# A third buffer for the conversion of a float64 weight, and a later place for the routing's constants

## The chip, the cores and the metric

The kernel runs on one core of a Trainium2 chip. The metric is the device time of one execution in microseconds; of several executions the median counts. The core has TensorE (matmuls into PSUM), VectorE, ScalarE and GpSimd for the work beside them, and SyncE, whose queue issues nearly all transfers of this kernel. Each engine takes its instructions in the order in which the program holds them.

## What is computed

Three blocks follow each other: an attention with a threshold, a dense two-layer block, and a routed block with 8 experts of which each token takes one.

```python
# attention: 4 x 8 heads, 576 positions, 64 wide; then x is [2304, 512]
scores = np.where(scores >= max(scores) - tau, scores, -1e9)
x = softmax(scores) @ v
# dense block, w_in [512, 2048], w_out [2048, 512], both float64 in memory
h = x @ w_in
g = np.where(h > 0, h, np.exp(np.minimum(h, 0)) - 1)
x = g @ w_out
# routed block, 8 experts, 512 -> 1024 -> 512
logits = x @ w_gate + modality_bias[modality_id]
e = argmax(logits); out = softmax(logits)[e] * (relu(x @ w1[e]) @ w2[e])
```

## The kernel before

The work is cut into three programs that follow each other: attention with the first dense layer (`Phase1`), the second dense layer with the routing (`Phase2`), and the experts (`Experts`). In the first two an order is worked out before the kernel is built: each step goes into a `Plan` with an engine, a cost, a due time, the steps it needs and the buffers it uses, and `Plan.order` lets a clock run over them. The step whose due time is earliest and whose buffer is free comes next on its engine. A ring (`pl.ring(tag, n)`) says how many buffers of a kind there are. The planner's times are only there to find an order; on the chip the engines take that order and wait for each other by semaphores.

High precision comes from splitting: a float32 operand becomes a high part and the remainder, and three matmuls stand for one product.

The change is in `Phase2`, in the stretch between the attention and the token stage. Four things run there side by side.

- **Units.** The first dense layer of the last batch: 32 units (two halves for each of 16 chunks of 128 hidden features), which I number 96 to 127 as the whole kernel counts them. A unit is 12 matmuls into one of six PSUM banks `u` (line 715), two ScalarE steps (`eh`: 727 and 731), one VectorE step (`g`: 734), which frees the bank, and a store of `g` to memory `gD` (738, 144 KB).
- **Conversion of w_out** (`convert`, chunk c = 0 to 15). w_out lies in memory as float64; a chunk is 128 rows, 512 KB. SyncE loads it (1152) into a buffer `gr`, of which there are two. VectorE makes a float32 pattern from the two halves of the bits (1162 and 1163, the bit steps), ScalarE the sign (1169) and the absolute value (1171), VectorE the product (1172), ScalarE the high part in `WB` (1174), VectorE the remainder (1175). The buffer is free again when 1163 and 1169 have read it.
- **Constants** (`constants`). Two groups share one buffer `stg`: the modality bias (two small loads at 1121 and 1122, VectorE 1128 to 1133), and the matrices for counting tokens (GpSimd iotas at 1096 to 1099, VectorE 1103 to 1108, then stores at 1112 to 1116: 128 KB to a table, one row, and three stores of 256.5 KB of zeros).
- **First pieces of g for the tokens** (`tokens`). There are 18 tiles of 128 tokens. Each takes its g in two halves of 8 feature chunks: a load of 512 KB into a buffer `gr` (1201), ScalarE's high part (1206), GpSimd's remainder (1210), then 24 matmuls (1227) of the 48 of a tile. Loads of g and chunks of w_out share the ring `gr`.

After the 18 tiles come the leading expert, whose rows are gathered into `XG0`, a tile of 128 x 2 x 513 floats that nothing uses before, and the other experts.

Of the kernel before, what the change touches and what calls it, by code (L numbers as in the profile page):

```python
# [11 lines left out]
I32 = mybir.dt.int32  # L12
# [195 lines left out]
class Phase1:  # L208
# [15 lines left out]
    def pools(self, ctx, xa, xb, tp):  # L224
        nc, tc, pl, o = self.nc, self.tc, self.pl, self.opt
        self.xa, self.xb, self.tp = xa, xb, tp
        pool = lambda name, bufs, **k: ctx.enter_context(tc.tile_pool(name=name, bufs=bufs, **k))
        one, self.wk, self.sm = pool("a1", 1), pool("awk", 1), pool("asm", 4)
        self.ps_s, self.ps_h = pool("ps_s", 2, space=PSUM), pool("ps_h", 4, space=PSUM)
        self.bufs = dict(s=2, h=4, e=2, p=o["p"], tf=2, th=2, tl=2, pvl=1, xo=o["xo"], R=1, qr=1, kr=1, ql=1,  # L230
                         vr=2, vs=2, kh=2, kl=2, q0=2, q1=2, eh=2, g=4, r=1, xha=1, xhb=1, w=1, wf=1, sums=4)
        for tag, n in self.bufs.items():
            pl.ring(tag, n, tag in ("vr", "vs", "q0", "q1"))
        self.ntau = one.tile([128, 1], F32, name="ntau")
        self.QS = [one.tile([128, 1280], F32R, name=f"QS{i}") for i in range(2)]

        self.VR = [one.tile([128, 5, 128], F32, name=f"VR{i}") for i in range(2)]
        self.VS = [one.tile([128, 5, 2, 64], F32R, name=f"VS{i}") for i in range(2)]
        for t in self.QS:
            nc.vector.memset(t[:, 576:640].bitcast(F32), 0.0)  # L240
# [815 lines left out]
class Phase2:  # L1056
# [14 lines left out]
    def pools(self, ctx, keep, xa, xb, tp):  # L1071
        tc, pl = self.tc, self.pl
        self.xa, self.xb, self.tp = xa, xb, tp
        one = self.one = keep.enter_context(tc.tile_pool(name="k1", bufs=1))
        pool = lambda name, bufs, **k: ctx.enter_context(tc.tile_pool(name=name, bufs=bufs, reuse_waits="tile", **k))
        self.sm, self.wk = pool("msm", 3), pool("gwk", 2)
        self.pu, self.pc = pool("ps_u", 6, space=PSUM), pool("ps_c", 1, space=PSUM)
        for tag, n in dict(u=6, xt=1, pr=1, xw=2, eh=2, g=4, gr=2, gs=2, stg=1, xrow=3, ht=1).items():
            pl.ring(tag, n, tag in ("gs", "ht", "xw"))
        self.XT0 = one.tile([128, 2, KT, 256], F32R, name="xt0")  # L1080
        self.XG0 = one.tile([128, 2, XW], F32, name="xg0")
        self.IDX = [one.tile([128, 24], I32, name=f"idx{i}") for i in range(2)]
        self.GT = [one.tile([128, 2], F32, name=f"gt{i}") for i in range(2)]
# [58 lines left out]
    def convert(self, c, t0, free):  # L1142

        nc, pl, T = self.nc, self.pl, self.T
        d = t0 + c * self.opt["wstep"]
        br = pl.new("gr")

        sl = c % 4 if c < 12 else 2 + c % 2

        def load():  # L1150
            T["w64", c] = self.wk.tile([128, 512, 2], I32, name="gr", tag="gr")
            nc.sync.dma_start(T["w64", c].rearrange("p a t -> p (a t)"), self.wsrc[:, c, :])

        raw = lambda w: T["w64", c][:, :, w]
        wf = lambda s: T["w64f"][sl // 2][:, sl % 2, s]
        dst = [self.WO[:, s, c, :] for s in range(2)]

        def bits():
            if c == 0:
                T["w64f"] = [self.xa.tile([128, 2, 2, 512], F32, name="w64f", tag=x, bufs=1) for x in ("xh", "xl")]  # L1160
            A = wf(0).bitcast(I32)
            nc.vector.tensor_scalar(A, raw(1), 0x08000000, 3, op0=ALU.bitwise_xor, op1=ALU.logical_shift_left)
            nc.vector.scalar_tensor_tensor(A, raw(0), 29, A, op0=ALU.logical_shift_right, op1=ALU.bitwise_or)

        ml = self.opt["wmul"](c)
        k0 = pl.dma(1456, 1, d - 4000, load, [], [br])
        before = self.slot.get(sl, [])
        k1 = pl.op("D", 1140, d, bits, [k0] + self.k_conv + before, [br], after=free, port=True)
        k2 = pl.op("A", 520, d, lambda: nc.scalar.activation(wf(1), raw(1).bitcast(F32), AF.Sign), [k0, *([k1] if c == 0 else []), *self.k_conv, *before], [br], after=free)
        self.k_conv = self.k_conv or [k1]  # L1170
        k3 = pl.op("A", 520, d + 1000, lambda: nc.scalar.activation(wf(0), wf(0), AF.Abs), [k1])
        k4 = pl.op(ml, 600 if ml == "D" else 1230, d + 1500, lambda: (nc.vector if ml == "D" else nc.gpsimd).tensor_tensor(
            wf(0), wf(0), wf(1), op=ALU.mult), [k2, k3], port=True)
        k5 = pl.op("A", 520, d + 2800, lambda: nc.scalar.copy(dst[0], wf(0)), [k4])
        k6 = pl.op("D", 600, d + 3300, lambda: nc.vector.tensor_tensor(dst[1], wf(0), dst[0].bitcast(F32), op=ALU.subtract),
                   [k5], port=True)
        self.slot[sl] = [k5, k6]
        self.wdone[c] = [k5, k6]
# [370 lines left out]
    def run(self):  # L1549
        o, pl, ph = self.opt, self.pl, self.ph  # L1550
        p1 = ph.pl
        t0 = max(p1.free["PE"], 0)
        self.wdone, self.l1mm, self.put3, self.k_w0, self.k_table, self.k_x = {}, [], [], [], [], []
        self.k_place = None
        self.k_conv = []
        self.slot = {}
        kneed = [max(p1.done(x) for x in y) for y in ph.xdone[B - 1]]
        tL = t0 + o["l1gap"]
        for u in range(2 * FC):
            self.l1mm.append(ph.unit(pl, B - 1, u, tL + 1464 * u, "u", self.pu, self.tp, [], kneed, []))  # L1560
            self.put3.append(len(pl.ops) - 1)
        self.constants(t0 + 10000)
        free = max(p1.done(k) for k in ph.last_mm)
        for c in range(FC):
            self.convert(c, t0 + o["w0"], free)
        t2 = tL + 1464 * 2 * FC
        self.gate_weights(t2)
        for i in range(TT):
            self.tokens(i, t2 + STEP * i)
            if i == PREDICT:  # L1570
                k = self.k_e0 = self.first(t2 + STEP * i + 18500)
                for c in range(8):
                    self.weights(c, k, t2 + STEP * i + 22000 + o["ew"] * c)
            if i == SNAP:
                self.begun(t2 + STEP * i + 18500)
        self.lead(t2 + STEP * TT)
        with self.tc.manual_schedule():
            pl.emit()
# [67 lines left out]
```

## Time and profile before

| | us |
|---|---|
| median of 3 runs | 1043.26 (1043.04 to 1044.56) |
| the profiled execution, its own time | 1040.67 |
| its span in the profile | 1038.7 |
| TensorE busy | 987.1 (95%) |
| VectorE busy | 633.5 (61%) |
| ScalarE busy | 566.5 (55%) |
| GpSimd busy | 472.2 (45%) |

The page gives shares over the whole span; a change in one stretch is read from that stretch. The units of the last batch run from 467 to 532 us of the span, the conversion of w_out from 471 to 536, the tokens from 533 to about 780, the experts from there to the end. In a timeline row the first number is the start, the second the duration of the group; in square brackets stands the idle time of the engine before it and what ended that. Consecutive instructions of one engine overlap a little at their ends, so their cost to the engine is the distance from one start to the next.

### The profile page before, as it was taken

The numbers are of one execution on the slowest core, as the hardware profiler recorded it, in microseconds if no ns is written. First come the engines' busy times: TensorE is split into PE (matmuls) and PEld (weight loads), VectorE is DVE, ScalarE is ACT, GpSimd is POOL, SyncE is SP. The second block draws the span as 40 slices with busy tenths as digits, with TensorE's granted clock in tenths as the row PEclk, the third lists the DMA queues.
The fourth block names the chain that finished last, engine by engine and source line by source line (L and its number), as shares of the span: only waits on it lengthen the run. The fifth ranks groups of instructions, "written<-read, shape, count | busy, mean of one in ns | idle before, by whom it ended". The sixth has DMA issues, their size and how long they took to land. (4 is left out here: it accounts for less than half of the span.)

```text
span 1038.7 us, 17784 instructions
## 1 busy us (share of the span) xinstructions
PE 987.1 (95%) x6241; PEld 864.3 (83%) x6241; DVE 633.5 (61%) x1574; ACT 566.5 (55%) x1183; POOL 472.2 (45%) x346
## 2 busy tenths in 40 slices
PE   8999899899999999998889999999999998999993
PEld 7666698899999999998778888877888897888982
DVE  6878899998989897856851222243444653464431
ACT  5777899899999999976762222333221211121000
POOL 3444787787667667541024444477523210211110
PEclk9999999999999999999999999999999999999997
DMA  5544454434424332116863333355312520441111
GB/s 174 152 121 128 118 152 132 123 117 118 131 88 123 99 111 70 59 64 199 227 211 113 105 104 103 114 153 172 112 41 83 200 65 24 141 122 53 41 44 25
DMA packets 107538, 117.75 MB, mean 113 GB/s; under 512 B 11920, under 2 KB 83872, under 8 KB 107426
## 3 DMA queue, kind: packets, MB, share of 16 engines
q1 hardware_dynamic: 102930, 104.00, 33.8%
q0 software_dynamic: 4496, 12.35, 3.9%
q8 instruction: 59, 0.97, 0.4%
q14 instruction: 53, 0.43, 0.1%
HBM read 80.36 MB, written 29.85 MB: 106 GB/s over the span
## 5 line engine op out<-in xcount | busy, mean ns | idle before, releaser
L1227 PE MATMUL u<-WB,gs 128*128 128x512 f32 x864 | 216.1, 402 | 3.7 <-POOL gs L1210 2.6
L1227 PEld LDWEIGHTS u<-WB,gs 128*128 128x128 f32 x864 | 158.4, 189 | 39.5 <-POOL gs L1210 3.7
L480 POOL TENSOR_TENSOR tl<-tf,th 128x512 fp32r<-128x512 f32 (+1 forms) x120 | 145.3, 1215 | 80.8 <-ACT tf L477 80.3
L715 PE MATMUL h<-xh,WA 128*128 128x288 f32 x768 | 172.4, 300 | 0.9 <-DVE g L734 0.5
L715 PEld LDWEIGHTS h<-xh,WA 128*128 128x128 f32 x768 | 128.8, 189 | 3.6 <-DVE g L734 1.9
L1210 POOL TENSOR_TENSOR gs<-gr,gs 128x1024 fp32r<-128x1024 f32 x36 | 87.1, 2420 | 95.2 <-ACT gs L1206 95.1
L419 DVE SCALAR_TENSOR_TENSOR p<-s,a,e 128x576 f32<-128x576 f32 x144 | 116.5, 813 | 19.5 <-ACT e L409 12.8
L397 DVE TENSOR_REDUCE a<-s 128x1 f32<-128x576 f32 x144 | 107.4, 753 | 16.4 <-PE s L386 14.1
L715 PE MATMUL h<-xl,WA 128*128 128x288 f32 x384 | 113.2, 295 | 0.0
L409 ACT ACTIVATE e<-s,a 128x576 f32<-128x576 f32 x144 | 106.8, 745 | 8.3 <-DVE a L397 6.4
L430 PE MATMUL h<-ident,p 128*128 128x128 f32 x576 | 87.8, 276 | 6.3 <-DVE p L419 4.9
L877 ACT CAST xtr<-px 128x512 fp32r<-128x512 f32 x16 | 9.4, 588 | 150.3 <-issue 85.2
L1258 DVE TENSOR_TENSOR lg<-xt,bt 128x8 f32<-128x8 f32 x18 | 3.0, 166 | 135.3 <-PE xt L1254 135.3
L820 POOL DMA_INDIRECT out<-o,idx x16 | 17.7, 1104 | 144.6 <-DVE o L932 101.3
L386 PE MATMUL s<-kh,QS 128*128 128x288 f32 x320 | 79.8, 331 | 1.4 <-DVE p L419 0.8
L430 PEld LDWEIGHTS h<-ident,p 128*128 128x128 f32 x576 | 68.8, 141 | 11.5 <-DVE p L419 4.7
L715 PEld LDWEIGHTS h<-xl,WA 128*128 128x128 f32 x384 | 72.6, 189 | 0.0
L386 PE MATMUL s<-kl,QS 128*128 128x288 f32 x320 | 69.1, 298 | 0.6 <-POOL kl L300 0.6
L1206 ACT CAST gs<-gr 128x1024 fp32r<-128x1024 f32 x36 | 37.8, 1049 | 56.5 <-issue 35.3
L471 ACT CAST th<-h 128x512 fp32r<-128x512 f32 (+1 forms) x120 | 64.0, 542 | 4.5 <-PE h L430 3.5
L477 ACT COPY tf<-h 128x512 f32<-128x512 f32 (+1 forms) x120 | 64.6, 546 | 1.4
L715 PE MATMUL u<-xh,WA 128*128 128x288 f32 x256 | 55.6, 306 | 8.6 <-DVE g L734 8.3
(207 smaller groups left out, 2083.7 us busy)
## 6 DMA issues: line engine op xcount, KB each, us to landing
gD<-g SPq DMA_DIRECT2D x128, 144.0 KB
gr<-gD SPq DMA_DIRECT2D x36, 512.0 KB
stg<-w SPq DMA_DIRECT2D x24, 512.0 KB
kr<-kP SPq DMA_DIRECT2D x30, 288.0 KB
w<-w_in SPq DMA_DIRECT2D x16, 512.0 KB
gr<-w_out SPq DMA_DIRECT2D x16, 512.0 KB
VR<-v SPq DMA_DIRECT2D x16, 320.0 KB
x2D<-xrow SPq DMA_DIRECT2D x18, 256.5 KB
```

What stands on the lines that cost most here:

```text
L386: nc.tensor.matmul(s[:, hf, 0:288], q, k[:, 288 * hf:288 * hf + 288], start=(m == 0), stop=(m == len(mm) - 1))
L397: nc.vector.tensor_reduce(T["a", i][:, 0:1], T["s", i][:, :, 0:288], axis=AX.XY, op=ALU.max, negate=True)
L409: nc.scalar.activation(e, T["s", i][:, :, 0:288], AF.Exp, bias=T["a", i][:, 0:1])
L419: nc.vector.scalar_tensor_tensor(p, T["s", i][:, :, 0:288], T["a", i][:, 1:2], T["e", i], op0=ALU.is_ge, op1=ALU.mult, accum_out=T["sums", ...
L430: nc.tensor.transpose(tp[:, 128 * c:128 * c + 128], pf[:, 128 * c:128 * c + 128], self.ident)
L471: a1 = op("A", ta(4), de, lambda src=src, dst=dst: nc.scalar.copy(dst("th"), src()), [k5], [bT])
L477: nc.scalar.copy(f[:, :, 0:w], src())
L480: nc.gpsimd.tensor_tensor(dst("tl"), T["tf", i, g][:, :, 0:w], dst("th").bitcast(F32), op=ALU.subtract)
L715: nc.tensor.matmul(T["h", key], self.WIN[:, s, kt, fc * 128:fc * 128 + 128], x[:, kt, q], start=(kt == 0 and j == 0), stop=(kt == KT - 1 a ...
L1206: nc.scalar.copy(T["gs", n % 2][:, 0], T["gr", n])
L1210: nc.gpsimd.tensor_tensor(g[:, 1], T["gr", n], g[:, 0].bitcast(F32), op=ALU.subtract)
L1227: nc.tensor.matmul(T["x2", i], T["gs", n][:, a, f % 8, :], self.WO[:, b, f, :], start=(f == 0 and j == 0), stop=(f == FC - 1 and j == 2))
```

## The change

The ring of buffers for chunks of w_out gets a third member for every third chunk (c = 2, 5, 8, 11, 14): the tile `XG0`, which later takes the leading expert's rows, is viewed as 1024 integers for each partition. In the plan the loads of chunks are due 4 us earlier and are counted as 1.5 us longer. The constants' due time moves from 10 to 46 us after the start of the stretch.

```diff
-        for tag, n in dict(u=6, xt=1, pr=1, xw=2, eh=2, g=4, gr=2, gs=2, stg=1, xrow=3, ht=1).items():
+        for tag, n in dict(u=6, xt=1, pr=1, xw=2, eh=2, g=4, gr=2, gs=2, stg=1, xrow=3, ht=1, xg=1).items():
...
-        br = pl.new("gr")
+
+        third = c % 3 == 2
+        br = pl.new("xg" if third else "gr")
...
         def load():
-            T["w64", c] = self.wk.tile([128, 512, 2], I32, name="gr", tag="gr")
+            if third:
+                T["w64", c] = self.XG0.rearrange("p a b -> p (a b)")[:, 0:1024].bitcast(I32).rearrange("p (a t) -> p a t", t=2)
+            else:
+                T["w64", c] = self.wk.tile([128, 512, 2], I32, name="gr", tag="gr")
             nc.sync.dma_start(T["w64", c].rearrange("p a t -> p (a t)"), self.wsrc[:, c, :])
...
-        k0 = pl.dma(1456, 1, d - 4000, load, [], [br])
+        k0 = pl.dma(1456, 1, d - 8000, load, [], [br], extra=1500)
...
-        self.constants(t0 + 10000)
+        self.constants(t0 + 46000)
```

The planner's order on TensorE stays as it was. On the others it changes within this stretch. In the kernel after the change the lines from 1152 on are numbered 5 higher (a load of a chunk is 1157, of g 1206).

SyncE's queue at the start of the conversion, before (`gr<-w_out` is the load of a chunk, `gD<-g` the store of a unit, `tabD` and the stores that follow it the constants):

```order
L1152 DMA gr<-w_out 128x1024 x2
L1121 DMA stg<-mod 128x18x2
L1122 DMA stg<-bias 128x16
L1184 DMA wg<-w_gate 128x4x8
L738 DMA gD<-g 128x288
L1152 DMA gr<-w_out 128x1024
L738 DMA gD<-g 128x288
L1152 DMA gr<-w_out 128x1024
L738 DMA gD<-g 128x288 x2
L1152 DMA gr<-w_out 128x1024
L738 DMA gD<-g 128x288 x2
L1152 DMA gr<-w_out 128x1024
```

and now (`xg` is the third buffer):

```order
L1157 DMA gr<-w_out 128x1024 x2
L1157 DMA xg_6987<-w_out 128x1024
L1121 DMA stg<-mod 128x18x2
L1122 DMA stg<-bias 128x16
L1189 DMA wg<-w_gate 128x4x8
L738 DMA gD<-g 128x288 x3
L1157 DMA gr<-w_out 128x1024 x2
L738 DMA gD<-g 128x288
L1157 DMA xg_6987<-w_out 128x1024
```

Chunk 2 is loaded right behind chunks 0 and 1, ahead of the small loads; chunk 3 stands behind three stores where chunk 2 stood behind one. Before, the constants' stores came right behind the last row shown, ahead of chunk 6.

The same queue at the end of the conversion, now, from the load of chunk 15 on:

```order
L1157 DMA gr<-w_out 128x1024
L738 DMA gD<-g 128x288
L1206 DMA gr<-gD 128x8x128
L738 DMA gD<-g 128x288 x4
L1206 DMA gr<-gD 128x8x128
L738 DMA gD<-g 128x288 x2
L1206 DMA gr<-gD 128x8x128
L738 DMA gD<-g 128x288 x2
L1112 DMA tabD<-stg 128x256
L1113 DMA x2D<-stg 1x513
L1116 DMA x2D<-stg 128x513 x3
L738 DMA gD<-g 128x288 x3
```

The constants' stores now stand behind the first three loads of g. The first load of g takes the buffer of chunk 13 (before: chunk 14's), the second the same buffer again once GpSimd has read it (before: chunk 15's), the third that of chunk 15.

VectorE behind the bit steps of chunk 15 (1167 and 1168), now:

```order
L1167 TENSOR_SCALAR w64f<-gr 128x512
L1168 SCALAR_TENSOR_TENSOR w64f<-gr,w64f 128x512
L1128 CAST stg<-stg 128x18
L1130 TENSOR_SCALAR stg<-stg 128x18
L1131 TENSOR_TENSOR bt<-stg 128x144
L1130 TENSOR_SCALAR stg<-stg 128x18
L1131 TENSOR_TENSOR stg<-stg 128x144
L1133 TENSOR_TENSOR bt<-bt,stg 128x144
L734 SCALAR_TENSOR_TENSOR g<-eh,u 128x288 x2
L1180 TENSOR_TENSOR WB<-w64f,WB 128x512
L1177 TENSOR_TENSOR w64f<-w64f 128x512
```

Before, the six rows of the bias stood behind the product of chunk 0, and the second group (1103 to 1108) behind the bit steps of chunk 3; that group now stands behind the remainder of chunk 15. The first of the two unit steps shown (734) is unit 121's, which frees the bank for unit 127, the last.

ScalarE at the same place, now:

```order
L727 ACTIVATE eh<-u 128x288
L1211 CAST gs<-gr 128x1024
L1174 ACTIVATE w64f<-gr 128x512
L1179 CAST WB<-w64f 128x512
L731 ACTIVATE eh<-eh 128x288
L1176 ACTIVATE w64f<-w64f 128x512
```

The cast of the first half of g (1211) now stands ahead of the sign of chunk 15 and of unit 121's exponential (731). Before, it stood behind the absolute value of chunk 15, one unit later.

## Rows read from the trace of the kernel before

**Rows 1.** Stretches: us, busy of PE, PEld, DVE, ACT, POOL, PEclk, DMA share, GB/s.

```profile
490.00:500.00 10.00, 7.19 (x48) 6.49 (x48) 6.34 (x13) 6.04 (x13) 0.00 (x0) 1.00 1.06 236
500.00:510.00 10.00, 8.33 (x51) 8.33 (x52) 9.50 (x19) 9.50 (x21) 0.00 (x0) 0.83 0.85 260
510.00:520.00 10.00, 9.22 (x65) 8.52 (x64) 9.01 (x18) 8.62 (x19) 0.00 (x0) 1.00 0.75 232
...
580.00:780.00 200.00, 197.15 (x998) 160.22 (x999) 65.64 (x308) 60.29 (x104) 102.74 (x54) 1.00 0.37 114
```

**Rows 2.** Waits from 466 to 540 us: us in total, times, longest.

```profile
ACT w64f L1169 <- DMA gr<-w_out: 8.9, 7, 3.4
PE u L715 <- DVE g L734: 8.3, 9, 3.9
```

**Rows 3.** Timeline of SyncE's queue: zeros, chunks 6 and 8, first and third g.

```profile
489.50 1.36 SPq L1116 DMA_DIRECT2D x2D<-stg  x3
...
491.82 0.63 SPq L1152 DMA_DIRECT2D gr<-w_out  x1
...
501.33 0.33 SPq L1152 DMA_DIRECT2D gr<-w_out  x1
...
525.88 0.37 SPq L1201 DMA_DIRECT2D gr<-gD  x1
...
535.19 0.37 SPq L1201 DMA_DIRECT2D gr<-gD  x1
```

**Rows 4.** Timeline of VectorE: chunk 0, bias, chunk 6, from chunk 13 on.

```profile
474.73 0.43 DVE L1162 TENSOR_SCALAR w64f<-gr 128x512 int32<-128x512 int32 x1 [5.52 <-DMA gr<-w_out]
...
478.20 0.17 DVE L1128 CAST stg<-stg 128x18 f32<-128x18 int32 x1
...
479.57 0.31 DVE L1133 TENSOR_TENSOR bt<-bt,stg 128x144 f32<-128x144 f32 x1
...
500.10 0.43 DVE L1162 TENSOR_SCALAR w64f<-gr 128x512 int32<-128x512 int32 x1 [3.24 <-DMA gr<-w_out]
...
522.12 0.69 DVE L1163 SCALAR_TENSOR_TENSOR w64f<-gr,w64f 128x512 int32<-128x512 int32 x1
522.73 0.45 DVE L734 SCALAR_TENSOR_TENSOR g<-eh,u 128x288 f32<-128x288 f32 x1
523.09 0.69 DVE L1175 TENSOR_TENSOR WB<-w64f,WB 128x512 fp32r<-128x512 f32 x1
523.70 0.45 DVE L734 SCALAR_TENSOR_TENSOR g<-eh,u 128x288 f32<-128x288 f32 x1
524.06 0.69 DVE L1172 TENSOR_TENSOR w64f<-w64f 128x512 f32<-128x512 f32 x1
524.66 0.42 DVE L1162 TENSOR_SCALAR w64f<-gr 128x512 int32<-128x512 int32 x1
525.12 0.69 DVE L1163 SCALAR_TENSOR_TENSOR w64f<-gr,w64f 128x512 int32<-128x512 int32 x1
...
529.33 0.45 DVE L734 SCALAR_TENSOR_TENSOR g<-eh,u 128x288 f32<-128x288 f32 x1
...
533.55 2.16 DVE L1175 TENSOR_TENSOR WB<-w64f,WB 128x512 fp32r<-128x512 f32 x1 [2.72 <-ACT WB L1174]
```

**Rows 5.** Timeline of TensorE: longest stand, last unit, tokens.

```profile
501.67 0.40 PE L715 MATMUL u<-xh,WA 128*128 128x288 f32 x1 [3.92 <-DVE g L734]
...
531.40 0.29 PE L715 MATMUL u<-xh,WA 128*128 128x288 f32 x1
...
535.22 16.66 PE L1227 MATMUL u<-WB,gs 128*128 128x512 f32 x70 [1.73 <-POOL gs L1210]
```

**Rows 6.** Timeline of ScalarE: the casts of the first and third load of g.

```profile
531.66 1.04 ACT L1206 CAST gs<-gr 128x1024 fp32r<-128x1024 f32 x1 [1.92 <-DMA gr<-gD]
...
540.49 1.05 ACT L1206 CAST gs<-gr 128x1024 fp32r<-128x1024 f32 x1 [1.28 <-PE u L1227]
```

**Rows 7.** Timeline of GpSimd: the remainder of the first half of g.

```profile
532.78 2.38 POOL L1210 TENSOR_TENSOR gs<-gr,gs 128x1024 fp32r<-128x1024 f32 x1 [52.25 <-ACT gs L1206]
```

## The prediction, made before the result was known

> **What bounds the kernel now.** I read the table of stretches first. In the token stage TensorE is busy for 197 of 200 us, so whatever starts that stage earlier moves everything behind it. Just before it, in the stretches from 490 to 520 us, TensorE is busy for only 7 to 9 us of each 10 [rows 1]. This is where the last 32 units of the first layer run beside the conversion of the 16 chunks of w_out. The waits say why: TensorE waits for a PSUM bank that VectorE's last step on a unit (L734) has to free, and VectorE and ScalarE themselves wait for chunks from memory [rows 2, 4]. The timelines give the case at its worst. The three stores of zeros from the constants are issued at 489.50, the load of chunk 6 at 491.82 behind them, and VectorE gets that chunk at 500.10, 8.28 us after its issue and after 3.24 us idle [rows 3, 4]. [...] Every engine works in its written order, so a late chunk holds the units' steps behind it.
>
> The units' last matmul ends at 531.7. Token 0 then needs its first half of g split in two: the load is issued at 525.88, ScalarE takes it at 531.66 after waiting for it, GpSimd starts at 532.78 and takes 2.38 us, and TensorE goes on at 535.22 without a further gap [rows 3, 5, 6, 7]. From there 70 matmuls in 16.66 us make 0.238 us each, so the 24 remaining before the second half's first product with a GpSimd part are over at 540.93. That point, third matmul of token 0's second half, is my yardstick; behind it TensorE alone sets the pace.
>
> **The change, part by part.** *Third buffer.* Loads go out for three chunks at once, not two. One buffer's turn is now the landing and 1.23 us until both readers are done (500.10 to the next issue at 501.33 [rows 3]). At the 5.78 us that the load at 525.88 took, a turn is 7.0 us: 3.5 us for each chunk with two buffers, 2.3 with three. VectorE needs more than the latter, so it becomes the bound. From rows that follow each other without a gap its steps cost, start to start: 0.46 and 0.61 for the two bit steps, 0.60 for the product, 0.61 for the subtraction, 0.36 for a unit's last step [rows 4]. In the new order there stand, from the first bit step to the end of chunk 13's: 14 pairs of bit steps (14.98), 13 products (7.80), 12 subtractions (7.32) and 19 units (6.84), 36.9 us in all. Chunk 0 lands when it did (474.73), because nothing before it moves. How much idle time comes on top I take from the stretch where loads hardly held it: from 500.10 to 529.33 stand 10 pairs, 10 subtractions, 9 products and 15 units, 27.6 us of work in 29.2, or 1.06. So chunk 13's bits end at 474.73 + 39.1 = 513.9; in the kernel before that was 522.73 [rows 4]. I call this point T; it comes 8.9 us earlier. Bounds: no idle time gives 511.7, the busy share of the stretch 510 to 520 (9.01 of 10 [rows 1]) gives 515.7.
>
> *Constants.* Their VectorE steps and stores leave the middle of the conversion. The modality bias (1.68 us from 478.20 to 479.88 [rows 4]) now stands behind chunk 15's bits, the other group behind the last subtraction. The zeros and the table's store then lie ahead of the load of token 1's second half. That load waits for GpSimd's second pass anyway (T + 18.8, below); with 5.78 us of landing its half is ready at T + 28.1 and wanted at T + 29.8, under the cover of 46 matmuls, so I count it at nothing; with 8.28 us it would be 0.9 us late. GpSimd's four iotas move between its first two passes, where it waits some 6 us.
>
> *From T to the yardstick.* The load of g's first half reuses chunk 13's buffer, so it goes out at T + 0.15 (before: behind chunk 14). With 5.78 us of landing, 1.12 us from ScalarE's start to GpSimd's and 2.38 us of GpSimd, the first half is ready at T + 9.4. TensorE is still on the units then: behind T VectorE has 4 units, 2 subtractions, 2 products, 2 pairs of bit steps and the bias, 7.7 us, before the step that frees the bank of the last unit, and ScalarE's cast of g, now ahead of that unit's exponential, holds it about 1 us more; the last unit ends 2.0 us after that step is over (529.7 to 531.7 [rows 4, 5]). So the units end near T + 11.2 and token 0's first 24 matmuls follow at once, to T + 16.9. But the second half's load waits for GpSimd to be done with the first (they share a buffer): issue at T + 9.5, landing 5.78, 1.12, and 2.44 from GpSimd's start to TensorE. That is T + 18.8, and later than T + 16.9: the gap at the start of the tokens is gone, and a new one of about 2 us lies in the middle of token 0. The yardstick comes at 513.9 + 18.8 = 532.7 instead of 540.93: **8.3 us earlier**.
>
> VectorE's subtraction of chunk 15 took 2.16 us beside GpSimd's pass, 0.61 elsewhere [rows 4, 7]. GpSimd's first pass now runs between T + 7 and T + 9.4, while VectorE still works for the units; one such hold of 1.5 us moves the first 24 matmuls to T + 18.4, still before T + 18.8, but it takes away what quicker landings could bring. [...]
>
> The profiled execution took 1040.67 us with a span of 1038.7, and the median is 1043.26. A shift in the middle changes neither of those differences: 1043.26 - 8.3 = 1035.0.
>
> **The rivals.**
> *Transfers become the bound.* VectorE's 2.8 us for each chunk ask for one chunk of 512 KB and about 1.5 stores of 144 KB, 728 KB or 260 GB/s. That is the most any stretch shows (260 at 500 us), and the stretch before was full at 236 GB/s with a share of 1.06 [rows 1]. If every load took the 8.28 us of chunk 6, a turn would be 9.5 us and three buffers 3.17 us for each chunk: T = 474.73 + 13 x 3.17 + 1.07 = 517.0, and the time 1038.2. Against it: that landing had the zeros ahead of it, which are gone. [...]
>
> *Only the constants count.* If the third load doesn't get ahead, since three stores of g now stand before the fourth load, what is left is the 3.24 us wait of chunk 6 and little else: 1043.26 - 3.6 = about 1039.6.
>
> *Slower.* Two loads of g now lie in series on the path, each issued only when GpSimd has finished or a chunk is read. Each microsecond that landing takes more costs two. The gain is gone at a landing of 5.78 + 4.15 = 9.9 us; at 11 us the kernel would be at 1045.5. For it: chunk 6's 8.28. Against it: 5.78 at 525.88, and the load issued at 535.19 had landed by 540.49, when ScalarE waited for TensorE, not for it: at most 5.3 [rows 3, 6].
>
> *Quicker.* With no idle time on VectorE (T = 511.7) and landings of 5.3, the path is T + 17.9 and the yardstick 529.6: 1031.9.
>
> A lost clock goes with all of these: the only fall in this stage came with a stand of 3.92 us, and 0.17 of 10 us are 1.7 us. The new stand is about half as long, so I leave it out of the forecast and put it into the range.
>
> **How the numbers follow.** The forecast of 1035.0 has 0.54, the quicker case 0.13, full transfers 0.16, the constants alone 0.06, an unseen cost that takes all of the gain 0.05, the serial loads 0.06. The range reaches from the quicker case to the slow T with the lost clock (515.7 + 18.8 + 1.7 = 536.2, a gain of 4.7, 1038.5), with half a microsecond beyond each: 1031.5 to 1039.0. It leaves out the constants alone, the last two cases, and a few hundredths of the others. About 0.2%, or 2.1 us, is what a measurement can tell from no change. Faster by more has the first four cases less 0.02, so 0.87; within it 0.07; slower 0.06.
>
> **What would show it.** T, the end of chunk 13's bits, near 514; no wait of VectorE or ScalarE for a chunk over 1 us behind chunk 3; no stand of TensorE of 3 us within the units; the first token matmul right behind the last unit; a stand of about 2 us before token 0's second half, ended by GpSimd; the yardstick near 533; and from there on the same distances as before. The forecast is wrong if chunks still arrive late (T near 517 or later), if either load of g takes over 8 us, or if the token stage behind shows gaps that it had not.

## The result and the profile after

The changed kernel takes 1032.92 us (median of four, 1030.96 to 1033.1) where the kernel before, run beside it, takes 1043.43 (1043.04 to 1044.56): a ratio of 0.9893 with a 95% interval of 0.9876 to 0.991, so 10.5 us less. The forecast was 1035.0. The profiled execution took 1032.86 us, with a span of 1030.8.

Before two traces are laid side by side, one has to see that they do not reach the stretch at the same time. SyncE issues the first two chunks at 470.75 in the kernel before and at 473.74 in this one, and the 2.99 us arise in the attention, which the change does not touch. In all 13 other profiles of this study that issue lies between 472.28 and 474.95, so it was the profile of before that was early. Below, I measure from that issue and call it the start.

The stretches, with [rows 1] as the counterpart (us, then the busy time of each engine, TensorE's granted clock, the share of the DMA engines, GB/s):

```profile
490.00:500.00 10.00, 8.49 (x62) 8.02 (x61) 9.61 (x20) 9.94 (x24) 0.00 (x0) 1.00 0.91 277
500.00:510.00 10.00, 9.82 (x72) 9.35 (x70) 9.90 (x20) 9.65 (x22) 0.00 (x0) 1.00 0.84 259
510.00:520.00 10.00, 9.03 (x64) 8.38 (x63) 9.86 (x21) 9.62 (x22) 0.00 (x0) 1.00 0.80 257
520.00:530.00 10.00, 7.05 (x51) 6.72 (x50) 9.79 (x20) 7.60 (x17) 2.88 (x5) 1.00 0.50 151
530.00:535.00 5.00, 5.00 (x23) 3.99 (x22) 2.78 (x10) 2.94 (x8) 2.43 (x1) 1.00 1.02 337
540.00:560.00 20.00, 19.27 (x91) 15.28 (x90) 2.62 (x18) 5.10 (x8) 8.35 (x4) 1.00 0.47 123
580.00:780.00 200.00, 197.37 (x1010) 160.94 (x1009) 62.56 (x301) 61.12 (x105) 102.29 (x54) 1.00 0.36 110
```

VectorE (third number) is now busy for 9.6 to 9.9 us of each 10 from 490 to 530: it has become the bound, and the hole of [rows 1] at 490 to 500, 6.34 of 10, is gone. No stretch of the conversion has less than the full clock. The waits from 466 to 540 us say the same (total, times, longest; counterpart [rows 2]):

```profile
PE u L715 <- DVE g L734: 5.8, 8, 3.0
ACT w64f L1174 <- DMA gr<-w_out: 2.3, 2, 2.1
DVE w64f L1167 <- DMA gr<-w_out: 1.6, 1, 1.6
```

VectorE waits for a chunk once, for chunk 3. TensorE still has one long stand. VectorE's timeline, from chunk 13's second bit step on, shows where it comes from (counterpart [rows 4]):

```profile
516.93 0.69 DVE L1168 SCALAR_TENSOR_TENSOR w64f<-gr,w64f 128x512 int32<-128x512 int32 x1
517.54 0.45 DVE L734 SCALAR_TENSOR_TENSOR g<-eh,u 128x288 f32<-128x288 f32 x1
...
523.95 0.31 DVE L1131 TENSOR_TENSOR bt<-stg 128x144 f32<-128x144 f32 x1
...
524.51 2.36 DVE L1131 TENSOR_TENSOR stg<-stg 128x144 f32<-128x144 f32 x1
...
527.13 0.81 DVE L734 SCALAR_TENSOR_TENSOR g<-eh,u 128x288 f32<-128x288 f32 x2
```

GpSimd's passes on g in the same trace (counterpart [rows 7]):

```profile
524.33 2.37 POOL L1215 TENSOR_TENSOR gs<-gr,gs 128x1024 fp32r<-128x1024 f32 x1 [50.62 <-DMA gD<-g]
...
532.14 2.43 POOL L1215 TENSOR_TENSOR gs<-gr,gs 128x1024 fp32r<-128x1024 f32 x1 [4.34 <-ACT gs L1211]
```

The step behind chunk 13's bits starts at 517.54, which is 43.8 us from the start; before it was 52.0. The product of the bias takes 0.31 us ahead of GpSimd's pass and 2.36 us beside it, and behind it stands the step on unit 121, whose bank TensorE needs for the last unit. ScalarE has its share in that too: it waits for the load of g and does unit 121's exponential only behind the cast:

```profile
523.20 1.05 ACT L1211 CAST gs<-gr 128x1024 fp32r<-128x1024 f32 x1 [1.60 <-DMA gr<-gD]
...
525.24 0.44 ACT L731 ACTIVATE eh<-eh 128x288 f32<-128x288 f32 x1
```

So the step on unit 121 could have started at 525.68 and starts at 527.13. Of the 2.05 us that the bias product is longer (2.36 less 0.31), 1.45 are on the path. TensorE's timeline (counterpart [rows 5]):

```profile
527.63 0.40 PE L715 MATMUL u<-xh,WA 128*128 128x288 f32 x1 [2.95 <-DVE g L734]
...
529.34 17.03 PE L1232 MATMUL u<-WB,gs 128*128 128x512 f32 x72
...
548.00 1.20 PE L1232 MATMUL u<-WB,gs 128*128 128x512 f32 x4 [0.73 <-POOL gs L1215]
```

The stand of 2.95 us lies ahead of the last unit. Behind it the tokens start without a gap, and the next stand, 0.73 us, is in the second half of token 1. Its load goes out at 535.51, behind the zeros of 532.03, and ScalarE has it at 544.42.

The stretch is not the whole gain. In the experts TensorE stood at one branch, before:

```profile
870.67 0.75 DVE L932 TENSOR_SCALAR o<-l,gr 128x512 f32<-128x512 f32 x1 [3.77 <-PE l L926]
...
873.73 5.98 PE L953 MATMUL l<-WA,xts 128*128 128x512 f32 x18 [3.10 <-DVEq L1008]
```

and after:

```profile
866.31 0.75 DVE L932 TENSOR_SCALAR o<-l,gr 128x512 f32<-128x512 f32 x1 [3.77 <-PE l L926]
...
867.27 4.45 PE L953 MATMUL l<-WA,xts 128*128 128x512 f32 x18 [0.99 <-DVEq L1008]
```

Line 1008 is a branch on the number of row blocks of the expert; DVEq is VectorE's sequencer, which releases TensorE with the first step behind the branch. That step comes 2.1 us sooner after VectorE's last instruction, and the 18 matmuls behind it take 1.5 us less, 3.6 us together. The prediction had nothing there.

From the start to TensorE's 152nd matmul, counted from the first token matmul with all kinds taken in, it is 96.3 us before and 88.8 after, 7.5 less; from there to the last matmul 454.6 and 451.1, 3.5 less. Those are the two places.

### The profile page after: what moved, and what is told of

Its sections match the earlier page's. It is cut to its first block, busy times and chain, and to the rows that moved or that the text cites. A ratio compares the mean times of both kernels' runs of the same rounds, so it can differ in the third digit from the quotient of the medians.

```text
span 1030.8 us, 17785 instructions
## 1 busy us (share of the span) xinstructions
PE 985.8 (96%) x6241; PEld 864.2 (84%) x6241; DVE 630.2 (61%) x1574; ACT 566.4 (55%) x1183; POOL 471.4 (46%) x346
## 5 line engine op out<-in xcount | busy, mean ns | idle before, releaser
L820 POOL DMA_INDIRECT out<-o,idx x16 | 17.7, 1104 | 144.7 <-DVE o L932 97.7
L386 PEld LDWEIGHTS s<-kh,QS 128*128 128x128 f32 x320 | 50.1, 194 | 15.9 <-issue 5.8
```

The source lines that it names most:

```text
L386: nc.tensor.matmul(s[:, hf, 0:288], q, k[:, 288 * hf:288 * hf + 288], start=(m == 0), stop=(m == len(mm) - 1))
```

## The experiments

Each ratio is to the kernel before, run in turn with it; before's medians were 1043.43 us beside after, and 1045.17, 1044.89, 1043.75 and 1043.88 in the four sittings that followed. Where I turn a ratio into microseconds I take it times 1043.43; the intervals are some 1.5 to 3 us to either side. The distances are from the start, in each profile, one execution of each kernel; T is the end of chunk 13's second bit step (0.1 us behind the start of the next step, by which the prediction counts), the yardstick the third matmul of token 0's second half, late the 152nd matmul from the first token matmul on. The stand is TensorE's ahead of the last unit, and the branch is the time from the matmul before the one at 867.27 to it.

| kernel | ratio (95%) | T | stand | first token | yardstick | late | branch |
|---|---|---|---|---|---|---|---|
| before | 1 | 52.1 | 0 | 62.0 | 70.2 | 96.3 | 3.50 |
| after | 0.9893 (0.9876 to 0.991) | 43.9 | 2.95 | 55.6 | 61.7 | 88.8 | 1.39 |
| after2 | 0.9894 (0.9869 to 0.9919) | 44.5 | 2.98 | 57.0 | 63.9 | 90.0 | 1.39 |
| e_pad4 | 0.9965 (0.9951 to 0.9979) | 52.0 | 0 | 62.0 | 71.7 | 97.7 | 1.39 |
| e_sub4 | 0.9925 (0.9899 to 0.9951) | 43.2 | 3.08 | 55.3 | 62.7 | 88.8 | 3.52 |
| e_const | 0.9972 (0.9955 to 0.9988) | 47.4 | 0 | 57.4 | 68.2 | 94.4 | 3.73 |
| e_third | 0.9926 (0.9904 to 0.9949) | 48.1 | 3.27 | 61.4 | 67.7 | 93.9 | 1.39 |
| v_a | 0.9899 (0.9878 to 0.9921) | 44.8 | 1.55 | 55.6 | 61.9 | 89.7 | 1.39 |
| v_d | 0.9952 (0.9935 to 0.9969) | 45.8 | 0 | 56.5 | 62.7 | 88.8 | 1.39 |
| e_zero | 0.9887 (0.986 to 0.9914) | 44.3 | 3.12 | 56.9 | 63.8 | 89.9 | 1.39 |
| x1 | 0.9881 (0.9852 to 0.9909) | 44.0 | 2.22 | 55.0 | 61.1 | 87.2 | 1.39 |
| x2 | 0.9903 (0.9878 to 0.9928) | 45.1 | 2.01 | 56.1 | 63.5 | 89.6 | 1.39 |
| x5 | 0.9887 (0.986 to 0.9914) | 45.0 | 2.00 | 55.9 | 63.4 | 89.5 | 1.39 |
| y7 | 0.9883 (0.9861 to 0.9904) | 44.9 | 0 | 53.7 | 61.9 | 89.6 | 1.39 |

### Where the experts' 3.6 us come from

The changed kernel has four VectorE instructions more than the kernel before. **e_pad4** gives the kernel before four:

```diff
+        pad = const.tile([128, 1], F32, name="pad")
+        for _ in range(4):
+            nc.vector.memset(pad, 0.0)
```

> The kernel before with four more instructions on VectorE, memsets of one element per partition at the very start; nothing else is moved. The changed kernel gained 3.6 us not in the stage that it edits but at one place of the experts: where TensorE starts the second half of the leading expert's rows it stood 5.98 us with VectorE's step behind a branch as the releaser, and 4.45 us (with less of it on VectorE) in the changed kernel, which has four more VectorE instructions ahead of that branch. Theory P, the place of VectorE's instructions relative to the blocks in which they are fetched: the stall shrinks here too, and the time is 3.6 us below the kernel before, ratio 0.9965. Rival Q, the shorter stall comes from what the change does to the work (earlier times, other traffic) or from chance: the ratio is 1.000 and the trace shows the stall of about 6 us again.

**e_sub4** takes four away from the changed kernel: the memsets of the two `QS` tiles (line 240) and those of `ones`, `ohs` and the table's padding, five in all, move to GpSimd, and one semaphore step comes back.

```diff
-            nc.vector.memset(t[:, 576:640].bitcast(F32), 0.0)
+            nc.gpsimd.memset(t[:, 576:640].bitcast(F32), 0.0)
...
+            nc.gpsimd.memset(self.ones, 1.0)
...
-            nc.vector.memset(self.ones, 1.0)
...
```

> The changed kernel with four VectorE memsets made by GpSimd instead (three of the routing's constants, and the zero columns of two tiles at the start, where a semaphore step comes back), so that VectorE has as many instructions ahead of the experts as in the kernel before; the orders around w_out's chunks are those of the changed kernel. Theory P (place of the instructions): the stall of about 6 us in the experts is back, the time is 3.6 us above the changed kernel, about 1036.5, ratio to before 0.9933. Rival Q: as the changed kernel, 1032.9, ratio 0.990.

Measured: 1040.6 us, 0.9965, and 1036.38 us, 0.9925, both as theory P had it. The interval of e_sub4 (0.9899 to 0.9951) just reaches the 0.990 of rival Q, so there the rows decide. TensorE's row at the branch in e_pad4:

```profile
875.22 4.44 PE L953 MATMUL l<-WA,xts 128*128 128x512 f32 x18 [0.99 <-DVEq L1008]
```

and in e_sub4:

```profile
868.69 5.97 PE L953 MATMUL l<-WA,xts 128*128 128x512 f32 x18 [3.13 <-DVEq L1008]
```

Four idle instructions at the very start of the program, 860 us earlier, take the stall away, and four fewer bring it back. So the edit's own steps have no part in it; the number of VectorE's instructions ahead of the branch does. What happens in the gap is in the list of DMA queues. From the start of VectorE's last instruction to its step behind the branch (870.7 to 873.6), before:

```profile
q14 instruction: 2, 0.02, 1.7%
```

From 865.6 to 868.6 in e_sub4:

```profile
q14 instruction: 2, 0.02, 1.8%
```

Two packets of 8 KB of instructions come through one queue while TensorE waits. In the gap of the changed kernel (866.3 to 867.2) no packet starts:

```profile
DMA packets 0, 0.00 MB, mean 0 GB/s; under 512 B 0, under 2 KB 0, under 8 KB 0
```

There a packet on that queue moved 4.5 us ahead of the branch (from 861.8 to 862.2):

```profile
q14 instruction: 1, 0.01, 8.6%
```

e_const and e_pad4 divide in the same way. e_const, with the long gap like before and e_sub4, has two packets of that queue in it (871.8 to 875.0); e_pad4, with the short one, has none in it (874.3 to 875.1) and one 4.5 us ahead of the branch (at 869.8). In the kernel before, none comes on that queue in the 25 us ahead of the branch. For the other nine profiles this is not shown.

That the two packets are what the step waits for in these 2.1 us is read from their place in time; no run held them back, and which numbers of instructions bring the stall is not shown. The other 1.5 us are matmuls at a lower clock behind the longer stand: from 860 to 890 us the granted clock is 0.94 in the kernel before and in e_sub4, 1.00 in the changed kernel and in e_pad4. (The later yardstick of e_pad4 in the table is the clock too, 0.83 from 535 to 545.)

So the edit is worth what e_sub4 shows, 0.9925 or 7.8 us (5.1 to 10.5 by its interval); 3.6 us (2.2 to 5.1 by e_pad4's) came by accident. Together that is 11.4, beside 11.2 by the changed kernel's own ratio.

### The two halves of the change apart

**e_const** is the kernel before with one line changed:

```diff
-        self.constants(t0 + 10000)
+        self.constants(t0 + 46000)
```

> Only the second half of the change: two buffers for the chunks as before, the constants made late. VectorE has as many instructions as before. If the third buffer is what keeps the chunks ahead of VectorE, this gives only the wait of chunk 6 behind the zeros (3.24 us): about 1040, ratio 0.9965, and the waits of VectorE and ScalarE for chunks stay, near 1.5 to 2 us apiece. Rival, the stores of the constants were the whole cause of the late chunks: the yardstick of the token stage comes some 7 us earlier as in the changed kernel, time about 1036, ratio 0.993. By theory P the stall of 6 us in the experts is in its trace either way.

**e_third** is the changed kernel with that line put back:

```diff
-        self.constants(t0 + 46000)
+        self.constants(t0 + 10000)
```

> Only the first half of the change: three buffers for the chunks, the constants where they were. If the third buffer is the cause of the gain in the stage, it takes the landing of chunk 7 behind the zeros (8 us where others take 5.8) without a long wait, VectorE does the constants' 3.3 us of steps inside the conversion, and since the bias is not made beside GpSimd's pass the units end about as early as in the changed kernel: the gain of the stage is 5 to 7.5 us. VectorE has six instructions more than the kernel before, for which theory P gives no sure sign: time 1036 to 1038.5 with the stall in the experts, 1032.5 to 1035 without. Rival, both halves are needed: a wait for a chunk of 3 us and more remains behind the zeros, the stage gains 3 us or less, and the time is above 1039.

Measured: 1042.68 us, 0.9972, and 1037.67 us, 0.9926. At T the halves give 4.7 and 4.0 us, 8.7 together, where the whole change has 7.6 to 8.9. So each half removes late chunks, more than one wait of 3.24 us, and they add up. In e_const VectorE waits for no chunk after the first and ScalarE 5.2 us in seven waits: the late chunks of the first half went with the stores, and my reading by chunk 6 alone was too small for T. The time gained little all the same, because the tail takes it back. The stretches of e_const there:

```profile
530.00:535.00 5.00, 2.11 (x7) 1.25 (x7) 3.12 (x6) 4.28 (x9) 2.38 (x1) 0.80 1.04 322
535.00:540.00 5.00, 5.00 (x14) 3.88 (x13) 0.56 (x2) 1.73 (x5) 2.40 (x1) 0.52 0.86 156
```

TensorE stands for GpSimd's pass as it did before, and then runs 5 us at a clock of 0.52; 14 matmuls fit where 23 fit at full clock (after, 530 to 535 us). That is more than 2 of its 4.7 us. In e_third chunk 7, which lands behind the zeros, costs VectorE 0.80 us, as the theory had it:

```profile
502.30 0.43 DVE L1167 TENSOR_SCALAR w64f<-gr 128x512 int32<-128x512 int32 x1 [0.80 <-DMA gr<-w_out]
```

But T is 4.2 us later there than in the changed kernel: these 0.8, 1.1 of a longer wait for chunk 3 (2.68 us, not 1.55), and for the rest, by subtraction, the constants' own steps on VectorE, which has no slack left to hide them. The tail is no shorter: from T to the first token it takes 13.3 us, where the four profiles with the changed order (after, after2, e_sub4, e_zero) have 11.7 to 12.6, with a stand of 3.27 and a clock of 0.83 from 530 to 540. In time, e_third without the 3.6 us of the branch has 4.1 us and e_const 2.9, together 7.0 beside the 7.8 of e_sub4, within the intervals. So the forecast for e_third (5 to 7.5 us in the stretch) was too high, and its rival (3 us or less) had the size at the yardstick, 2.5 us in one profile, by another mechanism than the wait it named.

### What holds the last unit

**after2** is the changed kernel again.

> The changed kernel again, unedited, as the measure for the other three of this chip and as a second look at where its time went. Expected: ratio to before 0.990 as at first; the same stand of TensorE of about 3 us ahead of the last unit, ended by VectorE's last step on a unit, with the bias product beside GpSimd's pass at 2.4 us where its twin takes 0.31; the same stand of 0.7 us in the second half of token 1; the shorter stall of 4.45 us in the experts. If the stand ahead of the last unit is an accident of one execution, it is under 1 us here.

It took 1034.39 us, 0.9894. The stand is there with 2.98 us, but this time it is the next step, `bt<-bt,stg` of line 1133, that takes 2.38 us beside the pass. The 0.73 us in token 1 are not, because token 0 ran slower: the clock from 530 to 535 is 0.78, not 1.00.

**v_a** makes the bias early again and keeps every step with two SBUF inputs behind the step on unit 121:

```diff
-        k = pl.op("D", 1800, t0, c2, [k], [bA])
+        k = pl.op("D", 1800, t0, c2, [k, self.l1mm[-1]], [bA])
...
-        self.k_bias = pl.op("D", 1530, t0, b1, [k0], [bB])
+        self.k_bias = pl.op("D", 1530, tb, b1, [k0], [bB])
...
-                   [k5], port=True)
+                   [k5, self.put3[25] - 2 if c == 14 else None], port=True)
...
```

> The changed kernel with the modality bias made early, as in the kernel before, the rest of the constants behind the last unit's matmuls, and the subtraction of chunk 14 behind the step on unit 121: so none of VectorE's steps with two inputs from SBUF stands ahead of the step that frees the last unit's bank. Theory H (GpSimd's pass holds such a step until it is over, but not the step on a unit, which has one input in PSUM): that step starts when its exponential is there, the stand ahead of the last unit shrinks from 3 us by 1.4 to 1.5, and the first token starts that much earlier; the second half of token 0 then waits about 1 us for its load in series behind the first (it was covered by 0.5 us in the changed kernel): net 0.5 to 1 us under the changed kernel. Theory S (the late point is ScalarE, which waits for the load of g and only then does the last exponential; the hold costs nothing): the stand stays near 3 us and the time is that of the changed kernel. If GpSimd's pass holds every step of VectorE, the step on unit 121 is itself 2 us long and the stand stays too.

It took 1034.72 us, 0.9899. In v_a GpSimd's pass runs from 525.19 to 527.60. VectorE's rows beside it:

```profile
526.55 0.45 DVE L734 SCALAR_TENSOR_TENSOR g<-eh,u 128x288 f32<-128x288 f32 x1 [2.11 <-ACT eh L731]
526.92 1.22 DVE L1180 TENSOR_TENSOR WB<-w64f,WB 128x512 fp32r<-128x512 f32 x1
```

The step on a unit, with one input in PSUM, runs through the pass in its usual 0.45 us. The subtraction behind it, with both inputs in SBUF, takes 1.22 us where it takes 0.69 elsewhere, and ends 0.54 us behind the pass. So the hold is of that kind, and theory H is right: the stand went from 2.95 to 1.55. What is left of it is theory S's part: the step on unit 121 comes after 2.11 us in which VectorE waits for ScalarE's exponential. Counted from T, the last unit starts 1.4 us earlier than in the changed kernel and the first token 1.0; 0.4 go to a new wait, for the bank of token 0's sums, which the step on unit 122 frees, and that stands behind the held subtraction. But T is 0.9 later than in the changed kernel's first profile (0.3 later than in after2), with the bias's steps (1.68 us in [rows 4]) ahead of it again, and token 1's second half now stands 1.26 us. No time was won.

**v_d** adds three moves to v_a: the third buffer takes other chunks, the constants' stores wait in the plan, and the first cast of g needs the exponential of unit 121 ahead of it (that edit is not shown here).

```diff
...
-        self.k_init = pl.dma(1500, 4, t0, c3, [k], [bA])
+        self.k_init = pl.dma(1500, 4, t0, c3, [k], [bA], after=t0 + 55000)
...
-        third = c % 3 == 2
+        third = c % 3 == 0
...
```

> The kernel of the early bias (the step on unit 121 ahead of the held ones) with three more moves: ScalarE's exponential of unit 121 stands ahead of the first cast of g, not behind it; the third buffer takes chunks 0, 3, 6 and on, so that the load of token 0's second half goes into chunk 14's buffer and is no longer in series behind GpSimd's first pass; and the stores of the constants go out after the first tokens' loads. Theory: no stand ahead of the last unit (the step that frees its bank can start near 523.6 of the changed kernel's trace), the first token starts when GpSimd's first pass is done, 2 us earlier than in the changed kernel, no stand in token 0 and none in token 1 (0.73 us): 2.7 us under the changed kernel, ratio to before 0.9875. Rival: the units were not what the first token waited for in the end, the cast of g moves later by what ScalarE does ahead of it, and the token starts within 0.5 us of where it did: only the 0.7 us of token 1 is won.

It took 1039.94 us, 0.9952, worse than the changed kernel by some 6 us. The stand ahead of the last unit is gone, but in v_d the hold has found another step (0.68 us elsewhere, here beside GpSimd's pass from 525.46 to 528.11), and TensorE waits at the first token:

```profile
525.94 2.72 DVE L1177 TENSOR_TENSOR w64f<-w64f 128x512 f32<-128x512 f32 x1
528.58 0.81 DVE L734 SCALAR_TENSOR_TENSOR g<-eh,u 128x288 f32<-128x288 f32 x2
```

So the first token starts at 56.5, no earlier, and the late mark is 88.8 as in the changed kernel. What costs the 6 us comes behind it, and it is the late stores. GpSimd, whose writes of tokens' places need the cleared table, in v_d from 576 us on:

```profile
576.74 1.16 POOL L1295 DMA_INDIRECT tabD<-ids,ri  x1 [1.33 <-DVE mx L1301]
583.93 0.96 POOL L1295 DMA_INDIRECT tabD<-ids,ri  x1 [6.03 <-DMA tabD<-ids,ri]
586.86 0.96 POOL L1295 DMA_INDIRECT tabD<-ids,ri  x1 [1.96 <-DMA tabD<-ids,ri]
587.84 4.69 POOL L1215 TENSOR_TENSOR gs<-gr,gs 128x1024 fp32r<-128x1024 f32 x2
```

Three such writes come at once and wait for each other, the passes on g queue behind them, TensorE stands for 4.41 us at 590.24, and the granted clock from 590 to 600 is 0.50 and 0.56. The constants' stores have a window, and 40 us later is past its end.

### The loads in series, and GpSimd's pass taken away

**e_zero** is the changed kernel with one edit of v_d alone (`third = c % 3 == 0`), so that the second load of g takes chunk 14's buffer.

> The changed kernel with one edit: the third buffer takes chunks 0, 3, 6 and on, not 2, 5, 8, so that the load of token 0's second half goes into the buffer of chunk 14 and no longer has to wait for GpSimd's first pass. The prediction said that these two loads in series set the yardstick. By the trace of the changed kernel they do not, by 0.5 us: the second half was ready at 534.6 and wanted at 535.0. Expected: the load goes out some 5 us earlier and the time does not change, within 0.5 us of the changed kernel. If the series did set it: 1 us or more faster.

The load goes out at 519.68, 6.6 us nearer to the start than in after2, and still the time is 1032.76 us, 0.9887, and the late mark 89.9 beside 90.0. The series of loads, on which the prediction's sum ended, does not bind in this order.

**x1** gives token 0's first subtraction to VectorE:

```diff
-                nc.gpsimd.tensor_tensor(g[:, 1], T["gr", n], g[:, 0].bitcast(F32), op=ALU.subtract)
+                (nc.vector if n == 0 else nc.gpsimd).tensor_tensor(g[:, 1], T["gr", n], g[:, 0].bitcast(F32), op=ALU.subtract)
...
```

> The changed kernel with the cause of the hold taken away: the subtraction of token 0's first half is made by VectorE (two of its 0.6 us steps in one, some 1.3 us), not by GpSimd, so that no pass of GpSimd runs while VectorE still works for the units. Theory H (the pass of 2.4 us holds whichever two-input step of VectorE comes next, 2.0 us each time): no step of VectorE is over 1.5 us between 520 and 531, the last unit starts about 1 us earlier and the first token with it; the time is 0.7 to 1 us under the changed kernel, ratio to before 0.9885. Rival: VectorE's own 1.3 us stand in the way of the units and eat what the hold cost: ratio 0.9894 as the changed kernel, the stand ahead of the last unit 3 us as before.

**x2** is x1 with `third = c % 3 == 0`; **x5** is x2 with the early bias and the order of v_a.

> The kernel with VectorE's subtraction, and beside it the third buffer for chunks 0, 3, 6 and on: the load of token 0's second half goes out without waiting for the first half to be used up. If the loads in series are what is late once the hold is gone, the second half of token 0 is ready some 3 us earlier here than in the kernel with VectorE's subtraction alone, and the time is up to 1 us under it; if the units still set it, the two are equal.

> The kernel with VectorE's subtraction and the third buffer for chunks 0, 3, 6, and besides the bias made early and the step on unit 121 ahead of chunk 14's subtraction. By the same rows the last unit starts 1.5 us earlier than in the changed kernel, the first token starts 1.5 us earlier, and neither token 0 nor token 1 stands for a load: 1.5 to 2 us under the changed kernel, ratio to before 0.9878. If the first token is then held by the cast of g (ScalarE waits for its load until 523.2 of the changed kernel's trace and then has four steps ahead of the units' exponential), half of it is left: 0.9886.

Measured: 1032.12 us (0.9881), 1033.63 (0.9903) and 1032.64 (0.9887). In x1 no step of VectorE from 520 to 531 us is over 1.23 us, the last unit starts 0.6 us nearer to the start than in the changed kernel and the first token too, and its late mark, 87.2, is the best of all. Of the stand of 2.22 us that is left, VectorE's own subtraction of 1.23 us has a small part: the exponential of unit 121 is over at 527.37 and its step starts at 527.73. The rest is ScalarE's, which had stood 1.95 us for the load of g. x2 and x5 start the first token 0.5 and 0.3 us behind the changed kernel's first profile and lose more to the clock, 0.73 and 0.66 from 530 to 535 us where x1 has 1.00. In time the three cannot be told from the changed kernel.

**y7** puts, in x2, the exponential of unit 121 ahead of the first cast, and the steps on units 122 and 123 ahead of chunk 15's product, both by a dependence in the plan (the second is shown):

```diff
...
-            wf(0), wf(0), wf(1), op=ALU.mult), [k2, k3], port=True)
+            wf(0), wf(0), wf(1), op=ALU.mult), [k2, k3, self.put3[26] - 2 if c == 15 else None], port=True)
...
```

> The kernel with VectorE's subtraction of token 0's first half and the third buffer for chunks 0, 3, 6 and on, with two orders changed: ScalarE does the exponential of unit 121 ahead of the first cast of g, for whose load it stands 1.9 us, and VectorE's steps on units 122 and 123 stand ahead of chunk 15's product. In the trace of the kernel with VectorE's subtraction the step on unit 121 started at 527.73, since ScalarE had waited for the load; the last unit's matmuls started at 528.24 after 2.22 us, the first token at 529.94. Theory (what is late once the hold is gone is ScalarE's wait for the load, ahead of the last exponential): no stand ahead of the last unit over 0.5 us, the last unit 2.2 us earlier, the first token 1.6 to 2.2 us earlier measured from the same matmul before the stage, and with no long stand no lost clock behind it: ratio to before 0.986 to 0.988. Rival: something else holds the first token (the cast of g, the subtraction, or the bank of unit 122), it starts within 0.7 us of where it did, and the ratio stays at 0.988 to 0.990.

It took 1032.86 us, 0.9883. The first part of the theory holds: no stand ahead of the last unit, and the first token starts at 53.7, 1.9 us earlier than in the changed kernel. Both causes of the stand are gone here, GpSimd's pass and ScalarE's wait for the load of g. Then TensorE meets, in y7,

```profile
535.06 12.57 PE L1232 MATMUL u<-WB,gs 128*128 128x512 f32 x46 [1.74 <-POOL gs L1215]
```

the stand that the prediction had put there: token 0's second half is not ready. Not for its load, issued at 521.19, but since ScalarE's cast waits until 531.44 for chunk 15's subtraction, whose scratch tile it takes, and that subtraction stands behind the bias:

```profile
531.48 1.05 ACT L1211 CAST gs<-gr 128x1024 fp32r<-128x1024 f32 x1 [1.17 <-DVE WB L1180]
```

The clock falls to 0.83 from 530 to 540, and the late mark is 89.6. Every repair of the tail moved the stand to the next step that was late. None of these versions beats the changed kernel by more than the measurement can tell.

## Why the prediction was right, and where not

**The bound (T).** Right. I had chunk 13's bits 43.2 us behind the start (513.9 less 470.75); the four profiles with the changed order (after, after2, e_sub4, e_zero; e_zero has the third buffer at other chunks) have 43.2 to 44.5. VectorE is full, transfers are not the bound: the stretch from 490 us moves 277 GB/s, more than the 260 that I took for the most.

**The loads of g.** Right in kind, a little too slow: from issue to ScalarE's start 5.50 and at most 4.28 us (517.70 to 523.20, 526.73 to 531.01), where the sum had 5.78 for each. That took the second half off the path: it is ready at 534.57, and its third matmul, the first that needs GpSimd's part, starts at 535.44. (The 535.0 in the expectations is the half's first matmul.)

**The stand.** The step that failed. I put a stand of 2 us into the middle of token 0 and saw none ahead of the last unit. My own sum has the step that frees the last bank at T + 8.7, and TensorE had work only until T + 7.1 (524.68), so some 2 us of stand lay there already. It measured 2.95 us. ScalarE's late exponential is in that sum: it is over at T + 8.1 (525.68), and v_a, without the hold, still stands 1.55. The hold is not: I priced it at 1.5 us and set it beside the path; it took 2.05, and 1.45 of them lay on the path. So the units end at T + 12.0, forecast T + 11.2, and they, not the loads in series, set the yardstick.

**The yardstick.** 61.7 us from the start, forecast 62.0 (532.7 less 470.75). That they agree is in part luck: the forecast has T + 18.8 by the loads in series, the kernel T + 17.9 by the units and 26 matmuls behind them, and T itself 0.6 later. After2 has 63.9: the same order, with a lower clock behind the same stand (0.78 from 530 to 535 us, 1.00 in after). The lost clock, which I left out of the forecast and put into the range with 1.7 us (the 0.83 of [rows 1], behind the 3.92 us of [rows 5]), does come in some executions.

**Token 1.** The forecast counted its second half at nothing, and at 0.9 us late if the load took 8.28 us; it took 8.91 behind the zeros (535.51 to 544.42) and was 0.73 late, in the execution that ran at full clock.

**Behind the yardstick.** Wrong: "the same distances as before" missed 3.6 us at one branch, of a kind that [rows 1 to 7] cannot show. The forecast of 8.3 us is near the edit's own 7.8 (e_sub4); the measured 10.5 holds the accident too. The range took it in by the room that I had left for quicker loads and a busier VectorE, which is not where it came from: luck again. With the edit's own ratio the time would be 1035.6, near the forecast.

**The rivals.** Full transfers and the serial loads are out by the rows above. The price of the first was wrong in itself: it charged 8.28 us to the chunks and left the two loads of g at 5.78; with 8.28 for both the same sum gives 540.8, no gain. Quicker (1031.9) came near in time, for another reason. That only the constants count is out too, since the third buffer gives 4.1 us by itself (e_third); the price of 3.6 us for the constants fits e_const's 2.9 (1.3 to 4.7), but at T they give 4.7, not one wait of 3.24.

## What to carry to other kernels

When two late sources feed one engine in order, each alone gives part of the gain (here 4.7 and 4.0 us at T) and the tail may take it back; ask what is late next with each half, not only with both. Where a GpSimd pass runs beside VectorE, list which of VectorE's steps with two SBUF inputs stand ahead of a step that TensorE waits for: here the next one in line took 2.36 us instead of 0.31 (after), 2.38 instead of 0.31 (after2), 2.72 instead of 0.68 (v_d). When a change adds or removes instructions ahead of a branch, compare the kernel with a padded copy of the one before, or a stall at the branch is booked to the edit, here 3.6 us.

## What the runs showed of the hardware

- Four memsets of one element per partition at the start of the program make it 3.6 us faster (0.9965, interval 0.9951 to 0.9979), by a branch 860 us later.
- The same stand of TensorE is followed by a lower clock in some executions and not in others: 2.95 and 2.22 us with 1.00 behind it (after, x1), 2.98, 2.01 and 2.00 us with 0.78, 0.73 and 0.66 from 530 to 535 us (after2, x2, x5). What decides it stays open.
- The start comes up to 2.7 us apart in executions with the same instructions ahead of it (472.28 in e_zero, 474.95 in x1), and at 470.75 in one.
- Beside a GpSimd pass of 2.4 us, a VectorE product of 128x144 with both inputs in SBUF takes 2.36 us instead of 0.31 (after); a step with one input in PSUM keeps its 0.45 (v_a).
